# Fewer unread products ahead of the keys, query features and a gate chunk moved in the opening of a linear-attention and SwiGLU kernel

## The chip, the cores and the metric

The kernel runs on one core of a Trainium2 chip. The metric is device time in microseconds (us) of one execution; less is better. Short names: PE is the matrix engine (TensorE), DVE VectorE, ACT ScalarE, POOL GpSimd, SP the engine that issues most of the loads. A time is about 1.7 us more than the span of the trace of the same execution. In each trace the first record of PE's full clock comes between 3.87 and 10.62 us; this moment is called the turn of the clock below. Starts of 512-wide products lie 0.43 us apart ahead of it in before.

## The reference

The inputs are random; batch 4, 4 heads, 1088 positions, head size 32, sketch size 8, feed-forward width 1536.

```python
def _attn_ref(q, k, v, S1, S2):
    def phi(x):
        a = np.einsum('rd,bhsd->bhsr', S1, x)
        b = np.einsum('rd,bhsd->bhsr', S2, x)
        return np.einsum('bhsi,bhsj->bhsij', a, b).reshape(*x.shape[:-1], r * r)
    q_p, k_p = (phi(q), phi(k))
    kv = np.einsum('bhsf,bhsd->bhfd', k_p, v)
    z = np.sum(k_p, axis=2)
    num = np.einsum('bhsf,bhfd->bhsd', q_p, kv)
    den = np.einsum('bhsf,bhf->bhs', q_p, z)[..., None] + 1e-06
    return (num / den).astype(np.float32)

def _moe_ref(x, w_gate, w_val, w_out):          # x: attention output, 4352 x 128
    g = x @ w_gate
    silu = g * (1.0 / (1.0 + np.exp(-g)))
    return (silu * (x @ w_val) @ w_out).astype(np.float32)
```

The sketches and the weights arrive as 64-bit numbers. The kernel makes 32-bit ones of them in three steps for each chunk: two DVE instructions, then two on ACT, then two on DVE and a product on POOL.

## The kernel before

Batch 0's attention is computed in the opening, ahead of any feed-forward product. From then on the feed-forward products fill PE, and the other batches' attention is woven in. These are the parts of the opening that matter here, each engine carrying out its own instructions in this order:

```python
    def keep_warm(n, w=TB, ps=None):            # n products that nobody reads, w columns wide
        if ps is None:
            ps = bank(free_banks[turn[0] % len(free_banks)])     # here always "g0"
        for _ in range(n):
            nc.tensor.matmul(ps[0:32, 0:w], warm[:, 0:32], warm[:, 0:w], start=True, stop=True)
    ...
    keep_warm(125, 32)
    ...                                         # S1, S2 to 32 bits: s32
    srep = bank("g0")                           # the sketch transposes write the same bank
    for h in range(H):
        nc.tensor.matmul(srep[...], s32[:], ident[0 : 2 * R, 0 : 2 * R], start=True, stop=True)
    keep_warm(6, ps=bank("acc"))                # six 512 columns wide
    nc.vector.tensor_tensor(out=s12[:], ...)    # reads srep
    for c in fpieces:
        turn_k(*c)                              # DVE: transposes of the keys
    prods = [key_products(...) ...]             # PE
    ...                                         # key features, their sums, query products
    nc.scalar.copy(zq[:], kz)                   # the sums of the key features
    qbs.append(query_copy(n, *pss[1]))          # ACT: one half of the second query pair
    key_values(kv, phk, *fpieces[0])            # PE: needs v
    key_values(kv, phk, *fpieces[1])
    phq = query_features(n, pss, qbs, pairs=(0,))
    ...                                         # zp: PE, from zq
    key_values(kv, phk, *fpieces[2])
    nc.vector.tensor_copy(zs[:], zp[:, 0:F])
    query_features(n, pss, qbs, phq=phq, pairs=(1,))
    ...                                         # kvs, zs turned by PE (L327): kvz
    part("wg", 0); part("wv", 0)                # ACT step of the first gate and value chunk
    turn_q(*steps[1])
    nd = totals(n, phq, kvz, ...)               # numerators and denominators: PE
    ...
    divide(0, *steps[0], nd, among=(("wg", 0), ("wv", 0)))   # dT, rc, rd, xT; DVE steps among them
```

## Time and profile before

| | before |
|---|---|
| time | 323.96 us, median of 3 (323.55 to 324.28) |
| span of the trace | 322.8 us |
| PE busy over the span | 97% |
| PE busy from 90 to 320 us | 228.3 of 230 us |
| first gate product starts | 17.42 us |
| PE gaps over 0.1 us, all | 5.0 us |

The traced execution is not among the three timed ones and is slower than all of them. The kernel is bound by PE nearly throughout, and 4.1 of the 5.0 us of gaps lie in its first 21 us. In the listings below a line reads: start in us, duration, engine, line of the kernel, operation, output and inputs, shapes, count, and in brackets how long the engine had been idle and what ended that. What follows can be read as one chain: keys, key features, their sums, turned sums, totals, division, first gate product.

### The profile page before, as it was taken

The page shows a single profiled execution, that of the slowest core. Times are in us where ns is not written, and L with a number is a line of the kernel's source. Part 1 is how long each engine was busy: PE and PEld are TensorE (multiplying, and loading weights), DVE is VectorE, ACT ScalarE, POOL GpSimd, SP SyncE. Part 2 cuts the span into 40 slices and gives each one's busy share as a digit, 9 for nine tenths or more (in the row PEclk, how much of TensorE's full clock was granted, in tenths as well). Part 3 has the DMA queues.
Part 4 walks back from the last instruction along what each step waited for, and adds up shares of the span by engine and source line. Part 5 has one row for each costly group of instructions (what it writes and reads, how often), then busy time and mean ns, then how long its engine had stood idle before and what let it go on. Part 6 is the DMA issues. An engine that isn't in the chain of part 4 may idle for free.

```text
span 322.8 us, 5580 instructions
## 1 busy us (share of the span) xinstructions
PE 313.2 (97%) x2288; PEld 189.9 (59%) x2288; DVE 156.6 (48%) x330; ACT 98.9 (31%) x227; POOL 37.6 (12%) x53
## 2 busy tenths in 40 slices
PE   8879999999999999999999999999999999999994
PEld 6535554656566665555666655555667655555672
DVE  3796889553465632454652543254544323322331
ACT  2457555421121322313222222223232222222220
POOL 2222333155000050000000060000000000000000
PEclk9999999999999999999999999999999999999998
DMA  7363390203132202100120100100010100100101
GB/s 206 105 196 99 120 264 19 71 0 79 19 68 48 69 2 69 26 0 2 22 75 0 22 2 0 25 1 2 0 26 0 19 1 2 25 0 0 24 2 20
DMA packets 25017, 13.99 MB, mean 43 GB/s; under 512 B 18848, under 2 KB 23072, under 8 KB 24992
## 3 DMA queue, kind: packets, MB, share of 16 engines
q1 hardware_dynamic: 24304, 13.56, 16.5%
q8 instruction: 18, 0.29, 0.3%
q10 hardware_dynamic: 688, 0.08, 0.2%
q14 instruction: 7, 0.06, 0.1%
HBM read 11.41 MB, written 2.23 MB: 42 GB/s over the span
## 4 chain that ended last, share of the span: by engine, by line
PE 90%; DVE 4%; ACT 2%; issue 1%; DMA 1%; POOL 0%; DVEq 0%
PE bank L513 50%; PE bank L541 28%; PE a L348 2%; PE a L398 2%; PE bank L194 2%; PE b L348 1%; PE a L304 1%; ACT exp L221 1%; DVE exp L216 1%; DMA raw<-in_moe_w_out_dram 1%; PE b L398 1%; PE a L273 1%; PE b L327 1%; DVE exp L224 0%; PE bank L316 0%
## 5 line engine op out<-in xcount | busy, mean ns | idle before, releaser
L527 DVE TENSOR_TENSOR hj<-sg,bank 128x384 f32<-128x384 f32 (+1 forms) x138 | 72.7, 529 | 122.5 <-PE bank L513 117.8
L519 ACT ACTIVATE sg<-bank 128x384 f32<-128x384 f32 (+1 forms) x144 | 67.7, 472 | 167.2 <-PE bank L513 165.6
L513 PE MATMUL bank<-xT,wg 128*128 128x384 f32 (+1 forms) x288 | 114.1, 478 | 2.7 <-POOL wg L232 1.1
L513 PE MATMUL bank<-xT,wv 128*128 128x384 f32 (+1 forms) x288 | 111.9, 470 | 0.3 <-DVE hj L527 0.3
L541 PE MATMUL bank<-hj,wo 128*128 128x384 f32 (+1 forms) x288 | 109.2, 471 | 0.1
L513 PEld LDWEIGHTS bank<-xT,wv 128*128 128x128 f32 x288 | 54.0, 190 | 35.2 <-DVE hj L527 3.6
L513 PEld LDWEIGHTS bank<-xT,wg 128*128 128x128 f32 x288 | 52.5, 190 | 37.1 <-issue 3.9
L541 PEld LDWEIGHTS bank<-hj,wo 128*128 128x128 f32 x288 | 54.0, 190 | 33.1 <-issue 2.4
L447 POOL TENSOR_TENSOR zs<-phk 128x1024 f32<-128x1024 f32 x3 | 7.1, 2353 | 107.1 <-PE bank L513 106.0
L376 DVE TENSOR_TENSOR phq<-a,qb 128x384 f32<-128x384 f32 (+1 forms) x11 | 5.8, 531 | 10.9 <-ACT qb L362 10.9
L362 ACT COPY qb<-a 128x384 f32<-128x384 f32 (+1 forms) x11 | 5.1, 461 | 15.4 <-PE b L348 8.6
L348 PE MATMUL a<-qT,sq 32*64 32x192 f32 (+1 forms) x176 | 9.2, 324 | 0.0
L348 PE MATMUL b<-qT,sq 32*64 32x192 f32 (+1 forms) x176 | 9.2, 324 | 0.0
L221 ACT ACTIVATE exp<-exp,rebias 128x384 int32<-128x384 int32 (+3 forms) x15 | 8.2, 548 | 3.0 <-DVE exp L216 2.3
L419 DVE STREAM_TRANSPOSE dT<-a 128x384 f32<-128x384 f32 (+1 forms) x8 | 4.4, 550 | 7.8 <-PE a L398 7.8
L362 ACT COPY qb<-b 128x384 f32<-128x384 f32 (+1 forms) x11 | 5.1, 463 | 9.2 <-PE b L348 5.4
L224 DVE SCALAR_TENSOR_TENSOR exp<-raw,exp 128x384 int32<-128x384 int32 (+2 forms) x14 | 7.4, 531 | 0.9 <-ACT exp L221 0.9
L348 PEld LDWEIGHTS a<-qT,sq 32*64 32x64 f32 x176 | 5.5, 131 | 3.9 <-issue 3.0
L376 DVE TENSOR_TENSOR phq<-b,qb 128x384 f32<-128x384 f32 (+1 forms) x11 | 5.8, 528 | 4.2 <-ACT qb L362 4.2
L557 DVE STREAM_TRANSPOSE o<-bank 128x384 f32<-128x384 f32 (+1 forms) x12 | 6.7, 561 | 2.2 <-PE bank L541 1.8
L232 POOL TENSOR_TENSOR wg<-man,exp 128x384 f32<-128x384 f32 (+2 forms) x5 | 4.6, 927 | 23.1 <-DVE man L228 18.0
L228 DVE SCALAR_TENSOR_TENSOR man<-raw,man 128x384 f32<-128x384 uint32 (+2 forms) x14 | 6.9, 493 | 0.0
(93 smaller groups left out, 165.6 us busy)
## 6 DMA issues: line engine op xcount, KB each, us to landing
kld<-in_k_dram SPq DMA_DIRECT2D x4, 544.0 KB, 4.3
vld<-in_v_dram SPq DMA_DIRECT2D x12, 144.0 KB, 3.9
qld<-in_q_dram SPq DMA_DIRECT2D x3, 544.0 KB, 4.0
raw<-in_moe_w_out_dram SPq DMA_DIRECT2D x4, 384.0 KB, 3.2
out_dram<-o SPq DMA_DIRECT2D x32, 48.0 KB, 1.8
raw<-in_moe_w_gate_dram SPq DMA_DIRECT2D x3, 384.0 KB, 3.3
raw<-in_moe_w_val_dram SPq DMA_DIRECT2D x3, 384.0 KB, 3.6
out_dram<-o SPq DMA_DIRECT2D x14, 40.0 KB, 1.7
```

What stands on the lines that cost most here:

```text
L221: nc.scalar.activation(e[:], e[:], AF.Relu, bias=rebias[: shape[0], :], scale=8.0)
L224: nc.vector.scalar_tensor_tensor(out=e[:], in0=hi, scalar=-(1 << 31), in1=e[:], op0=ALU.bitwise_and, op1=ALU.bitwise_or,)
L228: nc.vector.scalar_tensor_tensor(out=f, in0=lo, scalar=2.0**-52, in1=f, op0=ALU.mult, op1=ALU.add)
L348: nc.tensor.matmul(parts[g][F * half : F * half + F, t, 0:w], sq[r, t, :, :].rearrange("p i j -> p (i j)"), qT[r, x0 : x0 + n, half, :], s ...
L362: nc.scalar.copy(qb[:, :, 0:w], both[:, :, 1, 0:w])
L376: nc.vector.tensor_tensor(out=phq[:, 2 * pr : 2 * pr + 2, 0:w], in0=both[:, :, 0, 0:w], in1=qb[:, :, 0:w], op=ALU.mult,)
L398: nc.tensor.matmul(halves(nd[t])[half][32 * h : 32 * h + 32, 0:w], kvz[t][r, 32 * h : 32 * h + 32], phq[r, h, 0:w], start=True, stop=True,)
L447: add = lambda o, a, b: nc.gpsimd.tensor_tensor(out=o, in0=a, in1=b, op=ALU.add)
L513: nc.tensor.matmul(o[:, 0:n], w[:, j, :], xT[:, t0 : t0 + n], start=True, stop=True)
L519: nc.scalar.activation(sg[:, 0:n], g[:, 0:n], AF.Silu)
L527: nc.vector.tensor_tensor(out=hj[:, 0:n], in0=sg[:, 0:n], in1=u[:, 0:n], op=ALU.mult)
L541: nc.tensor.matmul(acc[i][:, 0:n], wo[:, j, :], hidden.pop((i, j))[:, 0:n], start=(j == 0), stop=(j == NCH - 1),)
```

## The change

The intent: get rid of unread products that hold up the keys, without letting PE's clock drop; let the query features use time in which DVE and ACT wait; take the gate chunk's DVE step out of the way of the division. The whole diff:

```diff
--- before.py
+++ after.py
@@ -420,15 +420,13 @@
             out=dT[:, 0 : 2 * n, :].rearrange("p (a x) t -> p a x t", a=2),
             in_=nd[1][:, :, 0:w].rearrange("p a (x t) -> p a x t", t=32),
         )
-        for p in among[:1]:
-            part(*p)
         nc.vector.tensor_scalar_add(rc[:, 0 : 2 * n], dT[:, 0 : 2 * n, 0], 1e-6)
         nc.vector.reciprocal(rc[:, 0 : 2 * n], rc[:, 0 : 2 * n])
         nc.vector.transpose(
             out=rd[:, 0 : 2 * n, :], in_=rc[:, 0 : 2 * n].unsqueeze(2).to_broadcast([P, 2 * n, 32])
         )
-        for p in among[1:]:
-            part(*p)
+        if among:
+            part(*among)
         xs = xT[:, t0 : t0 + 2 * w].rearrange("p (x a t) -> p a x t", a=2, t=32)
         rs = rd[:, 0 : 2 * n, :].rearrange("p (a x) t -> p a x t", a=2)
         if isinstance(nd[0], list):
@@ -567,7 +565,8 @@
 
 
 
-    keep_warm(125, 32)
+    keep_warm(98, 32)
+    keep_warm(18, 64)
     fills = {(w, i): narrow_w(w, i) for w in weights for i in range(len(pieces[w]))}
 
     def part(name, i):
@@ -587,7 +586,7 @@
             start=True,
             stop=True,
         )
-    keep_warm(6, ps=bank("acc"))
+    keep_warm(3, ps=bank("acc"))
     sTv = srep[:, 0 : 2 * R].rearrange("p (t r) -> p t r", t=2)
     nc.vector.tensor_tensor(
         out=s12[:],
@@ -620,11 +619,12 @@
     zq = apool.tile([P, H * F], FP32, tag="zq", name="zq")
     kvs, zs = (apool.tile([P, F], FP32, name=x) for x in ("kvs0", "zs0"))
     kvz = [apool.tile([P, P], FP32, name=x) for x in ("kvz0", "kvz1")]
+    qbs.append(query_copy(n, *pss[1]))
     nc.scalar.copy(zq[:], kz)
-    qbs.append(query_copy(n, *pss[1]))
+    part("wg", 0)
     key_values(kv, phk, *fpieces[0])
     key_values(kv, phk, *fpieces[1])
-    phq = query_features(n, pss, qbs, pairs=(0,))
+    phq = query_features(n, pss, qbs)
     zp = bank("g2")
     for h in range(H):
         nc.tensor.matmul(
@@ -633,22 +633,21 @@
         )
     key_values(kv, phk, *fpieces[2])
     nc.vector.tensor_copy(zs[:], zp[:, 0:F])
-    query_features(n, pss, qbs, phq=phq, pairs=(1,))
+    turn_q(*steps[1])
     for t, s, to, tag in ((1, zs, None, "g0"), (0, kvs, kv, "g1")):
         if to is not None:
             nc.vector.tensor_copy(s[:], to)
         ps = bank(tag)
         turn_kv(s[:], ps)
         nc.scalar.copy(kvz[t][:], ps[:, 0:P])
+    part("wv", 0)
     part("wg", 0)
-    part("wv", 0)
-    turn_q(*steps[1])
     nd = totals(n, phq, kvz, ([bank(t) for t in ("g2", "acc")], side_by_side("a")[0]))
     pss = query_products(*steps[1], ("b", ("g0", "g1")))
     qbs = [query_copy(steps[1][1], *ps) for ps in pss]
     turn[0] = 2
     keep_warm(3, ps=wide("a")[:, 0, :])
-    divide(0, *steps[0], nd, among=(("wg", 0), ("wv", 0)))
+    divide(0, *steps[0], nd, among=("wv", 0))
```

## The prediction

> **What bounds the kernel now.** I read the page first (engine shares, chain of work that ended last), then busy time by stretches, then the order-of-time listing of the first 25 us. The page says that the matrix engine is the bound, and the stretches say from when on. Columns after the stretch are its length, then busy time and count for PE, PEld, DVE, ACT and POOL.
>
> ```profile
> PE 313.2 (97%) x2288; PEld 189.9 (59%) x2288; DVE 156.6 (48%) x330; ACT 98.9 (31%) x227; POOL 37.6 (12%) x53
> 9.00:17.40 8.40, 7.03 (x205) 4.05 (x206) 6.64 (x24) 3.74 (x13) 2.25 (x3) 1.00 0.31 89
> 17.40:21.00 3.60, 2.55 (x36) 1.25 (x36) 3.56 (x13) 2.26 (x6) 1.18 (x2) 1.00 0.70 187
> 90.00:320.00 230.00, 228.32 (x1408) 140.21 (x1404) 97.76 (x190) 59.94 (x132) 10.14 (x8) 1.00 0.09 19
> ```
>
> From 90 us on PE is busy for 228.3 of 230 us, and nothing in the change touches that work. Only the opening can pay: up to the first gate product (17.42 us) PE waits for a chain through all engines, and between 17.4 and 21.0 us it is busy for 2.55 us while DVE is busy for 3.56. So the change is worth what it moves the first gate product and the DVE work behind it, and no more; each microsecond there should reach the end, since what follows hangs on the same order of instructions. The listing (start, duration, engine, line) carries the details:
>
> ```profile
> 0.85 3.49 PE L194 MATMUL bank<-const-bfloat16-1.0 128*32 128x32 bf16 x125 [0.85 <-PEq L756]
> 4.44 0.30 PE L583 MATMUL bank<-ident,s 16*32 16x16 f32 x8
> 4.68 2.44 PE L194 MATMUL bank<-const-bfloat16-1.0 128*32 128x512 bf16 x6
> 5.27 1.50 DVE L257 STREAM_TRANSPOSE kT<-kld 128x384 f32<-128x384 f32 x3 [0.17 <-DMA kld<-in_k_dram]
> 7.04 1.27 PE L273 MATMUL bank<-s,kT 128*64 128x64 f32 x36
> 7.93 0.95 DVE L293 TENSOR_TENSOR phk<-ka,bank 128x768 f32<-128x768 f32 x1 [1.17 <-ACT ka L287]
> ...
> 11.56 0.37 ACT L623 COPY zq<-bank 128x256 f32<-128x256 f32 x1 [0.54 <-PE bank L316]
> 12.52 0.61 DVE L382 TENSOR_TENSOR phq<-bank,qb 128x192 f32<-128x192 f32 x2
> 13.05 0.21 DVE L639 COPY kvs<-b 128x64 f32<-128x64 f32 x1
> 14.45 0.58 DVE L419 STREAM_TRANSPOSE dT<-a 128x384 f32<-128x384 f32 x1 [0.69 <-PE a L398]
> 14.95 0.25 DVE L224 SCALAR_TENSOR_TENSOR exp<-raw,exp 128x128 int32<-128x128 int32 x1
> 15.12 0.28 DVE L228 SCALAR_TENSOR_TENSOR man<-raw,man 128x128 f32<-128x128 uint32 x1
> 15.32 0.17 DVE L425 TENSOR_SCALAR rc<-dT 128x12 f32<-128x12 f32 x1
> 16.66 0.62 DVE L439 TENSOR_TENSOR xT<-bank,rd 128x192 f32<-128x192 f32 x2
> 17.42 0.88 PE L513 MATMUL bank<-xT,wg 128*128 128x384 f32 x2 [1.02 <-POOL wv L232]
> ```
>
> The reader is to see three things. The first keys are transposed at 5.27 + 0.54 = 5.81 us, yet the key products start at 7.04, because six unread wide products stand before them in PE's queue. The gate chunk's two DVE instructions (14.95, 15.12) stand between dT and rc, on the way to xT. And xT at 16.66 releases the first gate product.
>
> **What the Trainium skill says.** "TensorE: Matmul & The Clock Gate", Part 1 (the HAM clock gate), says the array starts at 1.2 GHz, and goes to 2.4 after a sufficiently busy, free-running window of 3413 ns. The trace agrees in effect: single starts of the 512-wide products lie 0.427 us apart (512 columns at 1.2 GHz), and the trace's first record of the full clock comes at 6.67 us; the 1.00 in the stretch view before it is only a default. So the unread products keep that window filled. Part 2 there (back-to-back issue gap) gives N/1.2 GHz for a cold array: 26.7 ns at 32 columns, as measured (125 starts, 26.7 ns apart); I estimate 53.3 ns at 64. Part 1's architectural detail says that ACT and DVE are strict FIFO; the order shown above agrees, and it is why moving instructions matters. "Perfetto Trace Analysis", per-instruction lifecycle, says that waits lie outside the reported durations, so I count from start to start.
>
> **The change part by part.**
>
> *Small products.* 98 of 32 columns and 18 of 64 replace 125 of 32. In array time: 98 x 26.7 = 2.62 us and 18 x 53.3 = 0.96 us, together 3.57 against 3.33 us, so 0.24 longer. Then the waits. Before, the last small product starts at 4.153, and the sketch transposes (L583) not until 4.444, 0.29 us after: in the trace PE's sequencer sits in a semaphore wait from 3.72 to 4.39 us. It waits for PE's own products, since both write the same bank (the sketch itself is ready at 3.65). In the compiled order of the changed kernel the first 64-wide product also waits on PE, for the same reason, and the sketch transposes wait again. So I do not believe "without a pause": I expect two. 98th start 0.85 + 97 x 0.0267 = 3.44; first 64-wide 3.44 + 0.27 = 3.71; 18th 3.71 + 17 x 0.0533 = 4.61; sketch transposes 4.61 + 0.29 + 0.03 = 4.93 us. **Cost 0.49 us.**
>
> *Wide products.* First one 0.23 us behind the sketch transposes, as before: 5.16. Three at 0.427 end at 6.44 instead of six at 7.0 (the sixth is partly warm). Key products 0.1 us later, as before: 6.54. By then DVE has made s12 at 4.88 + 0.49 = 5.37 and the first keys at about 6.15, so they no longer wait for DVE. **Net: 7.04 to 6.54, 0.50 us gained.** With the clock turning at 6.67 the first two pairs of key products are cold (0.05 us each lost), hence the first key features at about 7.45 instead of 7.93. I take **0.48 us**.
>
> *What follows to the key-value products.* They started at 10.92 us and would start at 10.44. They also need v; its last transfer is issued at 5.26 and takes 5.0 us: landed at 10.26, and not moved. So v is not yet in the way, but no more than 0.65 us could have been gained here.
>
> *Query features ahead of the sums' copy.* On ACT the two qb copies (0.55 us in all) go ahead of zq. Before, ACT idled 0.54 us before zq, so they fit: qb pair 0 ends at 10.04, pair 1 from 10.5 to 11.0; the sums are ready at 11.04 too, zq 11.04 to 11.4, and PE needs it at 10.44 + 1.05 = 11.49. Free. On DVE phq pair 1 (0.61 us) leaves the place before kvs, but turn_q (0.57 us) takes it: kvs 13.05 to about 12.53. **0.04 us beyond the shift.**
>
> *Gate chunk ahead of the division.* L224 and L228 leave the stretch from dT to rc. rc came 0.87 us after dT's start; dT itself is 0.58, and starts follow a dependent end by 0.03, so it can come after 0.61: **0.26 us gained.** In their new place, after kvs at 12.7, DVE waited 0.69 us for PE anyway, so they are hidden.
>
> Sum at the first gate product: 0.48 + 0.04 + 0.26 = **0.78 us**, 17.42 to about 16.64. DVE is near full from there to 21 us, and takes the shift along: the POOL product at 19.82 that ended PE's last long wait moves to about 19.04. Later loads are issued by the same chain and shift as well.
>
> **The rivals.** (1) *The clock turns late.* The two pauses and the short sketch transposes leave some 0.7 us of a window of 3.41 us idle (20%), against 0.45 before (13%, which sufficed) and about 30% in the window before it, which did not. If it misses, the next chance is at 10.1 us, and key, sum and query products run at half clock: 0.95 us more for key products alone, perhaps 1 to 1.5 us on the path, a loss of 0.3 to 0.8 in all. I give it 20%. (2) *The phase.* The window runs free of the kernel. Where the clock turns at 5.5 us, six wide products are cheap already (key products at about 6.5 before), and v's landing caps both kernels: the gain shrinks to 0.3 us. The spread of before, 323.55 to 324.28, fits such phases. A late turn makes it 0.9. Averaged I take about 0.55. (3) *v's landing takes the wait over.* It would if the second pause does not exist: the key products would start at 6.0, and v would hold the gain to 0.65 + 0.3, about 0.95 us in all. (4) *Nothing of it reaches the end*, if the weights' transfers bound the stretch of 30 to 53 us. Against it: there a transfer is issued when DVE has freed its buffer, so it moves along.
>
> **Range and chances.** With 323.96 before and 0.55 gained in a mean phase: 323.4. The low end takes the profile's phase, rival (3) and some noise (0.95 to 1.2): 322.7. The high end takes a late clock with half a microsecond lost: 324.4. 2% is 6.5 us, more than all idle time of PE in the opening (5.0 us of gaps over 0.1 us in the whole trace), so neither side is likely: 1% each.
>
> **What would show it.** Small products: the start of the sketch transposes (4.93; 4.43 if there is no pause). Wide: key products at 6.5 and the spacing of the wide ones. v: key-value products at 10.4, and whether PE waits for a DMA there. Gate chunk: start of rc less start of dT, 0.61. First gate product 16.6, POOL wg at 19.0. The prediction is wrong if the full clock's first record comes after 8 us, or if the gain at the first gate product is lost again before 60 us.

## The result

| | before | changed |
|---|---|---|
| median of 4 executions | 324.06 us (323.55 to 324.28) | 323.36 us (323.16 to 323.95) |
| span of the trace | 322.8 us | 321.5 us |
| clock turns to full, in the trace | 6.67 us | 5.38 us |
| first gate product | 17.42 us | 16.06 us |
| from the first gate product to the end | 305.41 us | 305.39 us |

The ratio is 0.9983, 95% interval 0.9968 to 0.9998. A ratio is the mean time of one kernel's runs over that of the other's in the same rounds, so it is not quite the ratio of the medians. By that interval there is a gain, but only just: it may be anything from 0.06 to 1.04 us.

The order-of-time listing of the changed kernel, with the lines that answer to those of before:

```profile
0.85 3.95 PE L194 MATMUL bank<-const-bfloat16-1.0 128*32 128x32 bf16 x116 [0.85 <-PEq L755]
4.90 0.30 PE L582 MATMUL bank<-ident,s 16*32 16x16 f32 x8
5.13 0.93 PE L194 MATMUL bank<-const-bfloat16-1.0 128*32 128x512 bf16 x3
5.47 1.49 DVE L257 STREAM_TRANSPOSE kT<-kld 128x384 f32<-128x384 f32 x3
6.09 1.58 PE L273 MATMUL bank<-s,kT 128*64 128x64 f32 x36
6.98 0.95 DVE L293 TENSOR_TENSOR phk<-ka,bank 128x768 f32<-128x768 f32 x1
...
10.36 0.88 PE L304 MATMUL b<-phk,vld 128*32 128x64 f32 x48
...
12.07 0.19 DVE L639 COPY kvs<-b 128x64 f32<-128x64 f32 x1
12.18 0.27 DVE L224 SCALAR_TENSOR_TENSOR exp<-raw,exp 128x128 int32<-128x128 int32 x1
...
13.34 0.58 DVE L419 STREAM_TRANSPOSE dT<-a 128x384 f32<-128x384 f32 x1 [0.69 <-PE a L398]
13.96 0.17 DVE L423 TENSOR_SCALAR rc<-dT 128x12 f32<-128x12 f32 x1
15.30 0.62 DVE L437 TENSOR_TENSOR xT<-bank,rd 128x192 f32<-128x192 f32 x2
16.06 0.88 PE L511 MATMUL bank<-xT,wg 128*128 128x384 f32 x2 [0.63 <-POOL wv L232]
```

The reader is to see three things. The sketch transposes come later than before (4.90 against 4.44), not earlier: PE waits for its own products twice. The keys' products start 0.95 us earlier all the same. And rc follows 0.62 us after dT, with L224 now far ahead of it.

This pair of traces flatters the change: it is 1.36 us ahead at the first gate product, twice the difference of the medians. The trace of before is of an execution of 324.56 us, slower than all four that were timed, and that of the changed kernel of one of 323.16 us, the fastest of its four. The clock turned 1.3 us earlier in the second trace, and that was not the change: in another trace of the same changed kernel it turned at 6.37 us (after_again below). The following table makes that visible for all traces (starts in us; the clock's turn and the landing of v's last transfer are read from the trace's own records). A label stands for an experiment below.

| trace | clock full | key products | key features | v landed | key-value products | copy kvs | dT | rc | first gate product | gate to end |
|---|---|---|---|---|---|---|---|---|---|---|
| before | 6.67 | 7.04 | 7.93 | 10.23 | 10.93 | 13.05 | 14.45 | 15.32 | 17.42 | 305.41 |
| changed | 5.38 | 6.09 | 6.98 | 10.26 | 10.36 | 12.07 | 13.34 | 13.96 | 16.06 | 305.39 |
| after_again | 6.37 | 6.48 | 7.37 | 10.26 | 10.36 | 12.46 | 13.73 | 14.34 | 16.45 | 305.37 |
| e1_gate | 6.11 | 6.77 | 7.66 | 10.27 | 10.65 | 12.78 | 14.18 | 14.79 | 16.89 | 305.38 |
| e2_warm | 5.76 | 6.17 | 7.06 | 10.13 | 10.22 | 12.18 | 13.58 | 14.45 | 16.55 | 305.37 |
| e3_query | 4.25 | 6.04 | 6.92 | 10.90 | 10.99 | 12.67 | 13.94 | 14.82 | 16.91 | 305.38 |
| e4_nopause | 6.37 | 6.14 | 7.12 | 10.16 | 10.26 | 12.20 | 13.48 | 14.09 | 16.20 | 305.41 |
| e5_early | 5.64 | 6.11 | 6.99 | 10.17 | 10.26 | 12.08 | 13.35 | 13.97 | 16.07 | 305.39 |
| e6_vfirst | 6.11 | 6.35 | 7.24 | 9.98 | 10.23 | 12.32 | 13.59 | 14.21 | 16.32 | 305.38 |
| e7_both | 5.14 | 6.01 | 6.90 | 9.73 | 9.90 | 11.98 | 13.25 | 13.87 | 15.98 | 305.41 |
| e8_cold | 10.62 | 6.00 | 7.23 | 9.30 | 11.24 | 13.33 | 14.61 | 15.22 | 17.33 | 305.38 |
| e9_wide3 | 4.24 | 5.87 | 6.75 | 11.01 | 11.10 | 12.78 | 14.05 | 14.67 | 16.78 | 305.40 |
| e10_nowide | 3.87 | 5.93 | 6.81 | 10.44 | 10.54 | 12.21 | 13.49 | 14.11 | 16.21 | 305.36 |
| e11_nosmall | 10.37 | 6.00 | 7.23 | 9.49 | 11.12 | 13.21 | 14.48 | 15.10 | 17.20 | 305.37 |

The last column is the firmest finding: in fourteen traces of thirteen kernels, the end lies 305.36 to 305.42 us behind the first gate product. Whatever moves that product moves the time by as much. The stretch before it is as steady: from the copy of kv to the first gate product it takes 4.37 us in before and e2_warm, 4.24 in e3_query, 4.11 in e1_gate, and 3.99 or 4.00 in the changed kernel and all that are built on it. So the moves of instructions are read from that stretch, and the rest (unread products, clock, v) from what lies ahead of it.

### The profile page after: what moved, and what is told of

Same layout as the page of the kernel before. It is cut to its first block, busy times and chain, and to the rows that moved or that the text cites. A ratio compares the mean times of both kernels' runs of the same rounds, so it can differ in the third digit from the quotient of the medians.

```text
span 321.5 us, 5554 instructions
## 1 busy us (share of the span) xinstructions
PE 312.6 (97%) x2276; PEld 189.9 (59%) x2276; DVE 156.7 (49%) x330; ACT 99.0 (31%) x227; POOL 37.6 (12%) x53
## 4 chain that ended last, share of the span: by engine, by line
PE 89%; DVE 5%; ACT 2%; issue 1%; DMA 1%; POOL 0%; DVEq 0%
PE bank L511 50%; PE bank L539 28%; PE a L348 2%; PE a L398 2%; PE b L348 1%; PE bank L194 1%; PE a L304 1%; ACT exp L221 1%; DVE exp L216 1%; DMA raw<-in_moe_w_out_dram 1%; PE b L398 1%; PE a L273 1%; PE b L327 1%; PE bank L316 1%; ACT man L222 0%
## 5 line engine op out<-in xcount | busy, mean ns | idle before, releaser
L224 DVE SCALAR_TENSOR_TENSOR exp<-raw,exp 128x384 int32<-128x384 int32 (+2 forms) x14 | 7.4, 532 | 0.9 <-ACT exp L221 0.9
```

The source lines that it names most:

```text
L224: nc.vector.scalar_tensor_tensor(out=e[:], in0=hi, scalar=-(1 << 31), in1=e[:], op0=ALU.bitwise_and, op1=ALU.bitwise_or,)
```

## The experiments

The theory after the result had three parts. First, each part of the change gives what its place in the chain gives. Second, the time varies with the turn of the clock. Third, v's landing stands close behind. The rivals: the gain was the clock's luck alone; or one part is the whole gain. Every experiment computed right results. "Before" was timed beside each, 324.01 to 324.11 us in the median (323.52 to 324.55). Edits are against the kernel that is named.

### e1_gate: the gate chunk alone (edit against before)

```diff
     qbs.append(query_copy(n, *pss[1]))
+    part("wg", 0)
...
-    part("wg", 0)
     part("wv", 0)
     turn_q(*steps[1])
+    part("wg", 0)
...
-    divide(0, *steps[0], nd, among=(("wg", 0), ("wv", 0)))
+    divide(0, *steps[0], nd, among=("wv", 0))
```

(and divide's two places for such steps made one, as in the change)

> Before with one part of the change alone: the gate chunk's ScalarE step right behind the query copies, and its two VectorE instructions ahead of the division. Theory (the parts add up, each on the path): from the start of dT to the start of rc 0.62 us instead of 0.87, the first gate product 0.26 us earlier at the same turn of the clock, the time 0.2 to 0.3 us below before. Rival (the shift is absorbed by PE's or GpSimd's later waits, or all of the gain came with the phase of the clock): rc moves but the time is within 0.1 us of before.

Measured: 323.68 us (323.36 to 323.98), ratio 0.9987 (0.9974 to 1.0001). DVE's listing in this trace:

```profile
12.78 0.21 DVE L638 COPY kvs<-b 128x64 f32<-128x64 f32 x1
12.91 0.57 DVE L263 STREAM_TRANSPOSE qT<-qld 128x384 f32<-128x384 f32 x1
13.40 0.25 DVE L224 SCALAR_TENSOR_TENSOR exp<-raw,exp 128x128 int32<-128x128 int32 x1
13.57 0.28 DVE L228 SCALAR_TENSOR_TENSOR man<-raw,man 128x128 f32<-128x128 uint32 x1
14.18 0.58 DVE L419 STREAM_TRANSPOSE dT<-a 128x384 f32<-128x384 f32 x1 [0.32 <-PE a L398]
14.79 0.17 DVE L423 TENSOR_SCALAR rc<-dT 128x12 f32<-128x12 f32 x1
```

DVE is still idle for 0.32 us ahead of dT, so the moved pair is hidden; rc comes 0.61 us after dT. From the copy of kv to the first gate product it takes 4.11 us against 4.37 before: 0.26, as predicted. The time alone would not have shown it, as its interval touches 1.

### e2_warm: the unread products alone (edit against before)

```diff
-    keep_warm(125, 32)
+    keep_warm(98, 32)
+    keep_warm(18, 64)
...
-    keep_warm(6, ps=bank("acc"))
+    keep_warm(3, ps=bank("acc"))
```

> Before with the unread products of the change alone (98 of 32 columns, 18 of 64, three wide). Theory: two waits of PE on itself, sketch transposes at 4.90 us instead of 4.44, key products at 6.0 to 6.6 instead of 6.1 to 7.3, depending on when the clock turns (5.4 and 6.7 us were seen); on average 0.25 to 0.3 us below before, up to 0.5 where the clock turns late. Rival 1 (this part is the whole gain): 0.7 us. Rival 2 (it costs as much in the sketch as it gains in front of the keys): within 0.1 us, and the first key features start no earlier than in before at the same turn of the clock.

Measured: 323.67 us (323.54 to 324.67), ratio 0.9998 (0.9985 to 1.0011). The medians say 0.36 us, the ratio 0.06; one execution in five at 324.67 makes the difference. By its time this is inconclusive. Its trace shows key products at 6.17 us with a clock that turned at 5.76, and the same 4.37 us from kvs to the first gate product as before.

### e3_query: the query features alone (edit against before)

```diff
-    nc.scalar.copy(zq[:], kz)
     qbs.append(query_copy(n, *pss[1]))
+    nc.scalar.copy(zq[:], kz)
...
-    phq = query_features(n, pss, qbs, pairs=(0,))
+    phq = query_features(n, pss, qbs)
...
-    query_features(n, pss, qbs, phq=phq, pairs=(1,))
+    turn_q(*steps[1])
```

(and the later turn_q taken out)

> Before with the move of the query features alone: the second pair's copies ahead of the sums' copy on ScalarE, its products ahead of the sums' on VectorE, the next transpose of queries ahead of the copy of kv. Theory: no instruction less, but the second turn of kv (L327) waits for VectorE alone and not for ScalarE as well, so that it starts 0.24 us after the copy of kv instead of 0.36: 0.12 us gained, time 0 to 0.15 us below before. Rival (zq, now behind two copies, comes late): zq starts later than 11.6 us and the time is 0.1 to 0.3 us above before.

Measured: 324.0 us (323.58 to 324.36), ratio 0.9999 (0.9987 to 1.0012). The second turn of kv starts 0.24 us after its copy, against 0.36, and 4.24 us lie between the copy and the first gate product against 4.37: the 0.13 us are there. But this trace showed something bigger. Its clock turned at 4.25 us, so the six wide products were cheap and the key features came at 6.92, a whole microsecond before those of before. PE's listing shows where that microsecond went:

```profile
10.99 0.88 PE L304 MATMUL b<-phk,vld 128*32 128x64 f32 x48 [0.48 <-DMA vld<-in_v_dram]
11.65 0.32 PE L630 MATMUL bank<-zq,sel 128*32 128x64 f32 x8
12.91 0.33 PE L327 MATMUL bank<-ident,kvs 128*64 128x128 f32 x2 [0.15 <-DVE kvs L639]
```

PE waits 0.48 us for v, which landed at 10.90. A gain in front of the keys can be taken back by a load.

### e4_nopause: no wait of PE for itself (edit against the changed kernel)

```diff
-    keep_warm(98, 32)
-    keep_warm(18, 64)
+    spare = wide("b")[:, 1, :]
+    keep_warm(98, 32, ps=spare)
+    keep_warm(18, 64, ps=spare)
```

> The changed kernel with its small unread products in a bank that the sketch does not use, so that PE waits for itself neither after the 98th nor after the last. Theory: sketch transposes at 4.45 us instead of 4.90, keys' transposes back at 5.27 (bound by the load of k), key products at 5.85 to 6.1; then v's landing (10.26) and zq stand close together, so 0.2 to 0.4 us below the changed kernel. Rival 1 (the pauses are harmless, the stage is bound by the keys' load and v): within 0.1 us of the changed kernel. Rival 2 (the clock's window): no pauses, so the clock turns no later than 6.7 us; if the idle share mattered to it, the spread of the times shrinks.

Measured: 323.34 us (323.24 to 323.44), ratio to before 0.998 (0.9968 to 0.9993). The sketch transposes start at 4.51 instead of 4.90, so the pauses were self-made: the bank that is written twice. PE's listing:

```profile
4.51 0.30 PE L583 MATMUL bank<-ident,s 16*32 16x16 f32 x8
6.14 1.28 PE L273 MATMUL bank<-s,kT 128*64 128x64 f32 x29
```

The key products start at 6.14 with a clock that turned at 6.37; the unaltered changed kernel had them at 6.48 with a turn at 6.37 (after_again). That is 0.34 us in the traces, which a mean of 323.34 against 323.34 us (nine executions of the changed kernel, from the result and after_again) does not confirm. By its time the expected 0.2 to 0.4 us did not come, and rival 1 stands: the pauses cost nothing that these times show. The spread is narrow (0.20 us), as rival 2 of the expectation put it, though five executions are few.

### after_again: the changed kernel once more

> The changed kernel unaltered, for a second trace and more times. Theory (the first gate product decides: in six traces the end lies 305.4 us behind it): again 305.4, and the key products start at 5.16 us plus three wide products, 6.5 us with a clock that turns at 6.7 or later, 6.1 with one that turns at 5.4; time 323.1 to 324.0 us. Rival (something behind the gate product varies between runs): the distance from the first gate product to the end differs by more than 0.2 us from 305.4.

Measured: 323.19 us (323.0 to 323.54), ratio 0.9976 (0.9964 to 0.9988). 305.37 us from the first gate product to the end. The clock turned at 6.37, and PE's listing reads:

```profile
4.90 0.30 PE L582 MATMUL bank<-ident,s 16*32 16x16 f32 x8
5.13 1.42 PE L194 MATMUL bank<-const-bfloat16-1.0 128*32 128x512 bf16 x3
6.48 0.92 PE L273 MATMUL bank<-s,kT 128*64 128x64 f32 x24
```

The three wide products take 1.42 us here and 0.93 in the first trace of the same kernel; the key products start at 6.48 against 6.09. Same program, other turn of the clock, 0.39 us at the first gate product.

### e5_early, e6_vfirst and e7_both: the two bounds lifted singly and together (edits against the changed kernel)

e5_early:

```diff
-    keep_warm(98, 32)
-    keep_warm(18, 64)
+    keep_warm(106, 32, ps=wide("b")[:, 1, :])
...
-    keep_warm(3, ps=bank("acc"))
+    keep_warm(4, ps=bank("acc"))
```

e6_vfirst (v's load, and the next part of q's, ahead of the first value chunk; that chunk's first DVE step later):

```diff
-        if i == 2:
+        if i == 1:
             load_v(0, [nc.sync] * 4)
...
     part("wg", 0)
-    part("wv", 0)
...
-    part("wv", 0)
     part("wg", 0)
+    part("wv", 0)
+    part("wv", 0)
     nd = totals(...)
```

e7_both has both edits.

> The changed kernel with 106 small products of 32 columns in a bank nobody waits for, and four wide ones: the sketch follows as soon as it is ready. Theory (the front is bound by PE's queue): sketch transposes at 3.75 us, key products at 5.9 at whatever turn of the clock, first key features at 6.85; then v's landing (10.1 to 10.9 us in the traces so far) holds the key-value products, so the time is only 0.1 to 0.3 us below the changed kernel. Rival (v's landing does not matter, PE's queue is all): 0.3 to 0.6 us below it. Rival 2 (the clock needs the second stretch of small products): the clock turns after 7 us and the time is above that of the changed kernel.

> The changed kernel with v's load ahead of the first value chunk's, whose first VectorE step moves behind the gate chunk's. Theory (v's landing, 10.1 to 10.9 us, bounds the changed kernel in runs where the clock turns early): v has landed by 9.6 us, no wait of PE for a DMA ahead of the key-value products, and the time is 0.1 to 0.3 us below the changed kernel, with fewer high times. Rival (not bound by v): the key-value products start when the sums are through, the gate product comes no earlier, same time within 0.1 us.

> Both of the two before together. Theory (two bounds stand close together, PE's queue in front of the keys and v's landing, so that lifting one alone pays little): first key features at 6.85 us, key-value products at 10.1, copy of kv at 11.9, first gate product at 15.9, time 322.9 to 323.1 us, 0.3 to 0.5 below the changed kernel and more than the sum of the two alone. Rival (the value chunk, now loaded later, becomes the new wait): its VectorE step waits for a DMA later than 12.3 us, and the time is not below e5_early.

Measured beside after_again (323.19 us, 323.0 to 323.54, mean 323.25):

| | median | lowest to highest | mean | ratio to before |
|---|---|---|---|---|
| e5_early | 323.63 | 323.21 to 323.94 | 323.55 | 0.9985 |
| e6_vfirst | 323.38 | 323.12 to 324.4 | 323.51 | 0.9984 |
| e7_both | 323.11 | 323.03 to 323.19 | 323.12 | 0.9971 |

Neither edit alone pays, so both expectations of 0.1 to 0.3 us were missed; if anything each was slower than after_again, but within the spread of single executions. In the traces, e5_early's key products came at 6.11 instead of 5.9, as k landed at 5.45, and e6_vfirst's v landed at 9.98 and not by 9.6. Together they give the lowest median, mean and spread. In e7_both's trace v landed at 9.73, the key-value products came at 9.90, and the moved value step found room where DVE waits anyway:

```profile
5.38 1.50 DVE L257 STREAM_TRANSPOSE kT<-kld 128x384 f32<-128x384 f32 x3 [0.94 <-DMA kld<-in_k_dram]
...
12.48 0.22 DVE L216 TENSOR_SCALAR exp<-raw 128x128 int32<-128x128 int32 x1
12.62 0.22 DVE L217 TENSOR_SCALAR man<-raw 128x128 int32<-128x128 int32 x1
13.25 0.58 DVE L419 STREAM_TRANSPOSE dT<-a 128x384 f32<-128x384 f32 x1 [0.42 <-PE a L398]
```

DVE idles 0.94 us for k ahead of the first transposes: k's landing, 5.35 us, is what bounds this version's front. My 5.9 us for the key products took k's landing of the first trace, 5.24; in fourteen traces it varied from 5.12 to 5.45, so 6.0 was to be had. e7_both beats before clearly (ratio interval 0.9958 to 0.9984). Over the changed kernel its lead is 0.13 us in the means, which these runs do not settle. That lifting both pays more than lifting one is likely: none of its five times is above 323.19 us, and of the eleven with one edit only one is below 323.21.

### e8_cold, e10_nowide and e11_nosmall: what the unread products are for (edits against the changed kernel)

e8_cold takes out all of them, e10_nowide the three wide ones, e11_nosmall the 116 small ones.

> The changed kernel without any unread product ahead of the keys. Theory (they are there to turn the clock, and the idle share of a window of 3.41 us decides): key products at about 6.1 us as soon as the keys are transposed, but at half clock, 1.9 us instead of 1.05; the clock turns after 9 us; the first gate product 0.5 to 1.5 us later than in the changed kernel at 16.1 to 16.5. Rival (the unread products only hold PE up): first gate product at 16.0, time as the best so far or below, 323.1 us.

> The changed kernel without the three wide unread products: PE idles from about 5.2 us to the key products at 6.1, 0.9 us more of the window. Theory (a window with more than some 13 to 30% idle does not turn the clock, as reckoned in the prediction): the clock turns after 8 us in some executions, the times spread by 1 us or more and their mean lies above the changed kernel. Rival (the small products suffice to turn it): clock before 6.7 us, key products at 6.1, times 323.1 to 323.6 us.

> The changed kernel without the 116 small products, the three wide ones kept. Question: v landed at 9.30 us in the trace without any unread products, at 10.1 to 10.3 in most with them, and at 10.4 to 11.0 in the three where the clock turned by 4.3 us. Theory (the array's unread work slows the loads, or something goes with it): v lands by 9.8 us. Rival (chance of that run): 10.1 us or later. Beside it, the clock: PE is idle up to the sketch at 3.95 us, busy from there to 8 us; theory of the idle share: it turns at 7.4 us or later, and the times lie between those of the changed kernel (mean 323.3) and those without unread products (324.4).

| | median | lowest to highest | mean | clock full in the trace |
|---|---|---|---|---|
| e8_cold | 324.42 | 324.04 to 325.05 | 324.41 | 10.62 |
| e10_nowide | 323.27 | 323.08 to 325.38 | 323.73 | 3.87 |
| e11_nosmall | 323.84 | 323.31 to 325.09 | 324.07 | 10.37 |

PE's listing of e8_cold, at the key products:

```profile
6.00 2.19 PE L273 MATMUL bank<-s,kT 128*64 128x64 f32 x36 [1.74 <-DVE kT L257]
8.33 1.07 PE L316 MATMUL bank<-phk,ones 128*32 128x256 f32 x6
```

The 36 key products take 2.19 us instead of 1.27 in before, the sum products 1.07 instead of 0.63: half clock. So without unread products the time is 1.07 us above the changed kernel (means 324.41 and 323.34; the ratios to before, 0.9997 to 1.0026 and 0.9964 to 0.9988 for after_again, do not overlap). By the means each kind helps, but for each kind alone this is not shown: the ratios to before are 0.9991 (0.9969 to 1.0012) for e10_nowide and 0.9998 (0.9979 to 1.0018) for e11_nosmall, and both intervals overlap with those of the changed kernel. Without the wide ones four executions of six were as fast as any, and two were at 324.28 and 325.38; without the small ones four of five lay at 323.8 or above. The traced execution of e10_nowide had an early clock, so that its two slow ones had a late one is inferred, not seen. In e11_nosmall's trace v landed at 9.49 us, as the theory there had it.

### e9_wide3: the old small products with three wide ones (edit against the changed kernel)

```diff
-    keep_warm(98, 32)
-    keep_warm(18, 64)
+    keep_warm(125, 32)
```

> The changed kernel with the small products of before (125 of 32 columns, one wait of PE on itself instead of two). Theory: sketch transposes at 4.45 us instead of 4.90, key products at 6.1 us even where the clock turns after 6.3 (6.48 in the changed kernel there), so 0 to 0.35 us earlier; v's landing then caps it, and the mean time is 0 to 0.2 us below the changed kernel: the small products' part of the change gains nothing. Rival (the wider small products help the clock turn earlier): the clock turns after 7 us in this trace or the mean time is 0.2 us or more above the changed kernel.

Measured: 323.35 us (323.18 to 323.88), ratio 0.9977 (0.9963 to 0.9992). The mean, 323.44 us, is 0.10 above that of the changed kernel: not to be told apart. In the trace the clock turned at 4.24 and the key products came at 5.87, the earliest of all. Its list of PE's waits between 8 and 13 us holds one for v:

```profile
PE b L304 <- DMA vld<-in_v_dram: 0.8, 1, 0.8
```

v landed at 11.01 us and took back all of it. So the reshaped small products are shown neither to help nor to harm the time; what the unread products gain must then come from the fewer wide ones, though no run took those alone.

## Why the prediction was right

The predicted 323.4 us stood against 323.36 measured, and a gain of 0.55 us in a mean phase against 0.70 between the medians (0.55 by the ratio). That it fits so closely is luck: the interval of the ratio allows 0.06 to 1.04 us, and after_again's ratio of 0.9976 says 0.78. What the runs bear out are the steps:

*Only the opening can pay.* Right: 305.36 to 305.42 us from the first gate product to the end, in all traces. Rival (4), that the gain is lost to the weights' transfers, is refuted by the same column.

*Two pauses in the small products.* Right: sketch transposes predicted at 4.93, measured at 4.90. In the trace of the changed kernel the last of 98 products starts at 3.43, the first 64-wide one at 3.68; e4_nopause, with another bank, has no such waits and starts them at 4.51.

*Key products at 6.54.* Right for the clock that it assumed: 6.48 in after_again, whose clock turned at 6.37. In the first trace it was 6.09, with a turn at 5.38. The key transposes did slip to 5.47, as the later sketch demanded.

*v's cap.* The mechanism was right, and e3_query and e9_wide3 show it at work, but the size was off. I put the stretch from the first key-value product to zp at 1.05 us, as in before; there, four of the key-value products start at 10.93, two sum products stand behind them in the listing and the other 44 start at 11.34. With PE held back only by v it was 0.66 to 0.69 us (10.36 to 11.05 in the changed kernel). So more than 0.65 us could be gained before v matters, and with v at 10.26 the sums' copy zq is just as late: zp waits for whichever ends last. In eight of the fourteen traces, both of the changed kernel among them, the first key-value product starts 0.09 to 0.10 us behind v's landing, so v is nearer than I thought. What I had not foreseen is that v's landing itself varies, from 9.30 to 11.01 us.

*Query features: 0.04 us.* These came: the copy of kv starts 0.53 us after the instruction in front of it before (phq, 12.52 to 13.05) and 0.49 us in the changed kernel (turn_q, 11.58 to 12.07). But 0.13 us more came behind that copy, by e3_query. (The working of the two copies also has a slip: by before's listing, moved by 0.48 us, pair 0 starts at 10.06 and ends at 10.54. Nothing hangs on it.) The term that I missed was not an instruction but a wait. Compare the second turn of kv. Before:

```profile
13.41 0.44 PE L327 MATMUL bank<-ident,kvs 128*64 128x128 f32 x4 [0.31 <-ACT kvz L642]
```

Changed:

```profile
12.31 0.44 PE L327 MATMUL bank<-ident,kvs 128*64 128x128 f32 x4 [0.15 <-DVE kvs L639]
```

It starts 0.36 us after the copy's start before and 0.24 after it now. In the traces' own records it waited for a semaphore of DVE and one of ACT, and now for DVE's alone. As I read the program, that is because it had to outlast the second pair's copies on ACT, which now stand ahead of zq, for which PE waits earlier. The kvz copy that the first listing names was not what it waited for: ACT's semaphore for it came at 13.42, when PE's weights for the turn were already loading (from 13.38); e1_gate and e2_warm show the same order.

*Gate chunk: 0.26 us.* Right: rc behind dT by 0.87, then 0.62 us; 0.26 us in e1_gate.

*Late clock, one in five.* It was not seen in the two traces of the changed kernel, and none of its nine times is over 323.95. The idle share was a fair guide. In after_again the window that ended with the turn, taken as 3.41 us long, has about 0.62 us (18%) without an unread or sketch product, and the clock turned. Before's window ahead of its turn had 29% (counted as idle up to PE's first product, from 0.15 us ahead of the trace's start), and one of e11_nosmall's, 3.54 to 6.95, had 32%, and neither turned it. The bound lies between, if it is the idle share at all.

*The phase* (when the clock turns). Right, and by the estimate below it makes up some 0.6 of the 1.36 us by which the first two traces differ. Of the 1.36 us between them, 0.38 lie behind the copy of kv (0.26 and 0.13, rounded), which are the program's. The other 0.98 are unread products together with the clock. At equal turns I estimate the unread products' share from the products' own pace: before's key products would start at 6.1 + 0.5 x (6.37 - 4.68) = 6.9 us with a turn at 6.37 (six wide ones from 4.68, 0.22 us apart when fast, as in the changed kernel's trace, and about twice that when slow, with 0.1 us behind them), and after_again has 6.48, so some 0.4 us. With the 0.38 that is close to the predicted sum of 0.78. The same rule gives 6.8 for e1_gate's turn at 6.11, measured 6.77; for three wide ones from 5.13 it gives 6.2 at e2_warm's turn (5.76) and 6.4 at e6_vfirst's (6.11), measured 6.17 and 6.35. It also says when the unread products gain nothing: with a turn before 4.7 us, six of them leave the key products at 6.1 (e3_query, 6.04), and in the changed kernel the keys' first transpose, from 5.47, leaves no earlier start than about 6.05.

## What to carry to other kernels

When a kernel is dense behind its opening, time one instruction, the first of the dense part, and count every change by how far it moves that. Before trusting two traces that differ by a microsecond, look at when the clock turned and when the loads landed in each, compare the times of the traced executions with the medians, and take a second trace of the same program. Unread products earned their place here by turning the clock, so end them when the data arrives; a bank that nobody else needs soon spares PE's wait for itself, though here that moved the sketch by 0.39 us and not the time. When a gain in one chain does not show, look for a second wait that ends just behind it, and try to lift both together.

## What the Trainium skill lacked or had wrong

- "TensorE: Matmul & The Clock Gate", Part 1, says that a busy window turns the clock, but not how busy. Here a window with about 18% of its time idle turned it (after_again, 6.37 us), and windows with about 29% (before) and 32% (e11_nosmall) did not; that the idle share decides is not shown. The page's advice that the ramp is below 1% of a kernel holds: going without unread products cost 1.07 us of 324, 0.3%.
- I found on no page that v's landing goes with the clock. The clock turned after 10.3 us in two traces, and v landed at 9.30 and 9.49; turned at 5.3 to 6.7 with the same order of loads (seven traces), 10.13 to 10.27; turned by 4.3 (three traces), 10.44, 10.90 and 11.01. The three groups do not overlap, and the cause is open: unread products, the array's pace, or something that decides both.
- I found on no page that PE waits for its own products when two groups write one bank and nobody reads it: 0.24 us from the last of 98 products to the first of the next group against 0.027 within one, and 0.29 us before in front of the sketch. In these kernels it comes as a semaphore wait in the program.
- "Perfetto Trace Analysis", Identifying Dependency Chains, says that a wait on several engines may be given an instruction of its own, without a cost. Here it was about 0.09 us: PE's turn started 0.15 us after the end of the copy with two engines waited for, 0.05 with one (before and changed). The other 0.03 of the 0.12 us between the starts is the copy's own length, 0.21 against 0.19.
